# Power-of-two scales from square sums and ones-matmuls, two weights read once, and a stored rank for every operation

## Chip, cores and metric

One core of one Trainium2 chip. The metric is the device time of one launch in microseconds. The engines are TensorE (PE, its weight loads are listed as PEld), VectorE (DVE), ScalarE (ACT), GpSimd (POOL) and the queue of SyncE (SP), which issues most DMAs.

## What is computed

Three stages follow each other on 8 sequences of 576 tokens, 512 wide.

```python
scores = q @ k.T / sqrt(64)             # 8 batches, 8 heads, 576 x 64
scores = where(block_i >= block_j, scores, -1e9)   # blocks of 64 tokens
x = softmax(scores) @ v                 # heads side by side: 576 x 512
gate = sigmoid(sum_k conv_w[k] * shift(x, 4 - k))  # 5 taps along the tokens
y = (gate * (x @ w_val)) @ w_out
xk = mu_k * y + (1 - mu_k) * prev(y)    # prev: one token earlier
xr = mu_r * y + (1 - mu_r) * prev(y)
out = sigmoid(xr @ w_r) * (square(relu(xk @ w_k)) @ w_v)
```

q, k, v and the two mu are float32, the five weights float64. w_val, w_out and w_r are 512x512, w_k is 512x1024, w_v is 1024x512.

## The kernel before

**Numbers.** Every product is taken three times in float16: each operand is scaled by a power of two, split into a high and a low half (h, l), and h·l, l·h and h·h are added in PSUM. So each operand needs a bound from which its power of two is taken. `layer` (line 1086) issues such a product, in weight pieces of 64 columns (line 1095).

**Pairs.** Attention works on 32 pairs of heads, four to a batch (p = 0 to 31). `attention_in` (line 947) loads q and k of a pair, `scales` (line 833) finds the bounds, `split` (line 865) makes the halves, a DMA transpose and two DMA copies put them in place. `attention_s` (line 991) does nine score tiles: matmuls (897), row maximum on DVE (903), exponential on ACT (906), then the probabilities in halves (584, 582, 594), and a DMA transpose. `attention_out` (line 1033) multiplies by v (942), then the five taps on DVE (1049), and splits x.

**Bounds before.** For q and k of a pair the sum of absolute values of each partition is taken, on ACT or DVE (826, 828), for v a sum of squares on ACT (847). `spread` (line 614) takes the maximum over the partitions to all of them: a matmul against the float32 identity (622), a maximum on DVE (624), a small diagonal (597), a matmul with ones (628). Bit operations (600, 605), a limit, a reciprocal and a last scaling give the scale. Each chunk's xk goes the same way with one column (from line 1205).

**Weights.** A block is 128 rows x 512 columns; there are 28: 4 of w1 (w_val), 4 of w2 (w_out), 8 of w3 (w_k), 4 of wr, 8 of wv. A block of float64 comes in as pairs of 32-bit words into one of four staging places (parts of tg and xx). It is made float32 by one scaling (`rescale`, 582 or 584) and three integer steps on DVE (650, 652, 656). For w1, w2 and w3 (`weights_by_sum`, line 731) the float32 block is stored, its absolute values (742) are summed over the rows by matmuls with ones (744), and the maximum gives the scale; then come a scaling, the high half (line 727) and the subtraction that makes the low half (591). For wr and wv, `bound_of_max` (line 756) reads each block and takes a maximum on DVE (610, into wmx); after the fourth pair `weights_by_max` (line 782) reads every block a second time and scales it within the first conversion step.

**Chunks.** After attention the tokens go in 13 chunks of 384 or 192 through `chunk` (line 1119): V (x by w1), O (by w2), Z (by wr), K (by w3) and W (by wv), all on PE, with their splits on the other engines.

**Order of the work.** Nothing is issued where it is written: `plan.add` records each operation with a label, a rank, a cost, the engines that may do it, and what it reads and writes. `Plan.order` (line 78) walks through a model of the engines: on each one that is free it starts the ready operation of the lowest rank, on an operation's preferred engine (table PREF), or on another one once it has waited for its patience (PATIENCE). `plan` (line 245) did this three times, and took the ranks of the second and third from `latest` (line 201), which walks backwards from the end, plus offsets by label and some nudges. Labels with a prime belong to the first pairs and first chunks (`plan.mark`, line 1358). Each engine's instructions, and the DMAs of each queue, stand in the order so found.

Of the kernel before, what the change touches and what calls it, by code (L numbers as in the profile page):

```python
# [7 lines left out]
F32 = mybir.dt.float32  # L8
# [24 lines left out]
class Plan:  # L33
# [5 lines left out]
    MODE = {"S": 1, "pv": 1, "xT": 2, "xB": 3}  # L39
    BANKS = {"sp": (0, 1), "xps": (2,), "xt": (2, 2), "xb": (2, 2), "fp": (3, 4, 5)}  # L40
# [37 lines left out]
    def order(self, off={}, patience={}, pref={}, base=None, stay=0.0):  # L78
# [6 lines left out]
        rank = [((base[n] if base else o[1]) + off.get(o[0], 0.0), n) for n, o in enumerate(ops)]  # L85
# [50 lines left out]
        for _ in ops:  # L136
            while True:
# [10 lines left out]
                if ops[n][6] == 2:  # L148
# [3 lines left out]
            n = min((rank[x][0] + (stay if e == PE and mode[x] != last else 0.0), x)  # L152
                    for x, r in waiting[e].items() if r <= t and when(x, r, e) <= t)[1]
# [44 lines left out]
        self.span = [o[2][0][1] if o[6] else finish[n] - start[n] for n, o in enumerate(ops)]  # L198
        return sorted(range(len(ops)), key=lambda n: (start[n], n))

    def latest(self):
        ops, finish, TO = self.ops, self.finish, self.TO
        where = [SP if o[6] else e for o, e in zip(ops, self.taken)]
        users = [[] for _ in ops]
        for n, o in enumerate(ops):
            for d in o[3]:
                users[d].append(n)
        left = [len(u) for u in users]
        free = {e: 0.0 for e in (PE, DVE, ACT, POOL, SP, None)}
        waiting = {e: {} for e in free}  # L210
        back = [0.0] * len(ops)

        def ready(n):
            t = float(self.DMA_OUT) if ops[n][6] else 0.0
            for u in users[n]:
                if where[n] == where[u] == PE:
                    x = back[u] - self.DRAIN
                else:
                    x = back[u] + (0 if ops[n][6] or where[n] is None else TO[where[u]]) + (self.DMA_SET if ops[u][6] else 0)
                t = max(t, x + (self.DMA_OUT if ops[n][6] else 0))  # L220
            waiting[where[n]][n] = t

        for n in range(len(ops)):
            if not left[n]:
                ready(n)
        for _ in ops:
            best = None
            for e, w in waiting.items():
                if w:
                    t = max(free[e], min(w.values()))  # L230
                    if best is None or t < best[0]:
                        best = (t, e)
            t, e = best
            n = -min((self.end - finish[x], -x) for x, r in waiting[e].items() if r <= t)[1]
            del waiting[e][n]
            back[n] = t + self.span[n]
            free[e] = t + (self.span[n] - self.DRAIN if e == PE else max(60.0, self.span[n] - self.OVER.get(e, 0.0)))
            for d in ops[n][3]:
                left[d] -= 1
                if not left[d]:  # L240
                    ready(d)
        end = max(back)
        return [end - x for x in back]

    def plan(self):
# [1183 lines left out]
```

## Time and profile before

| | us |
|---|---|
| median of 3 runs (1041.07 to 1041.95) | 1041.94 |
| the profiled execution | 1043.63 |
| its span, first to last instruction | 1041.8 |
| PE busy | 887.8 (85%) |
| DVE busy | 860.8 (83%) |
| ACT busy | 696.8 (67%) |
| POOL busy | 556.1 (53%) |
| mean granted clock of PE | 0.966 |

Read it by stages: busy shares over the whole span hide that the engines take turns in being full. 1.00 of the granted clock is 2.4 GHz, 0.5 is 1.2 GHz.

### The profile page before, as it was taken

How to read it: one execution, taken by the hardware profiler on the slowest of the kernel's cores; microseconds unless marked ns; L12 is line 12 of the kernel's file. 1: busy time of each engine (PE TensorE's matmuls, PEld its weight loads, DVE VectorE, ACT ScalarE, POOL GpSimd, SP SyncE). 2: the span in 40 equal slices, each digit the busy share in tenths (PEclk: the TensorE clock that was granted, in tenths of full speed). 3: DMA queues.
4: the chain of work that ended last, by engine and by line, in shares of the span. 5: the costliest groups of instructions: out<-in, count | busy, mean ns of one | idle time of the engine just before them, and what ended most of it. 6: DMA issues, size and time to landing. Idle time of an engine off the chain costs nothing.

```text
span 1041.8 us, 31117 instructions
## 1 busy us (share of the span) xinstructions
PE 887.8 (85%) x12195; PEld 628.3 (60%) x12195; DVE 860.8 (83%) x2095; ACT 696.8 (67%) x1607; POOL 556.1 (53%) x1097
## 2 busy tenths in 40 slices
PE   1335337999988999999998999999999989999998
PEld 0122226667666776756665767676666867675774
DVE  5899899999999998688898996878999986866341
ACT  3758577767878777567686876577787764652431
POOL 3655655645566746366466464355667462652321
PEclk9996568999999999999999999999999999999999
DMA  7988996267987985277976946349789860440000
GB/s 238 221 248 210 218 229 166 57 128 169 178 171 149 181 147 103 58 131 152 167 136 147 185 93 118 84 111 199 146 152 166 164 130 11 113 85 12 12 22 26
DMA packets 417203, 141.51 MB, mean 136 GB/s; under 512 B 403488, under 2 KB 403488, under 8 KB 417056
## 3 DMA queue, kind: packets, MB, share of 16 engines
q1 hardware_dynamic: 414368, 130.08, 61.2%
q0 software_dynamic: 2688, 9.45, 2.7%
q8 instruction: 95, 1.56, 0.7%
q14 instruction: 52, 0.43, 0.1%
HBM read 49.31 MB, written 9.44 MB: 56 GB/s over the span
## 4 chain that ended last, share of the span: by engine, by line
PE 42%; DVE 17%; DMA 5%; ACT 4%; issue 3%; POOL 2%; SPq 1%; ACTq 0%; DVEq 0%; POOLq 0%
PE fp L1095 35%; DVE P L594 3%; PE xps L942 3%; DVE tg L1049 3%; DVE smalls L903 2%; DMA rawq<-in_q_dram 2%; PE spa L897 2%; PE spb L897 1%; DMA q2T<-qkT 1%; POOL smalls L597 1%; ACT P L906 1%; DVE kx L594 1%; DMA PT<-P 1%; DVE natqk L594 1%; DVE tmp L1280 1%
## 5 line engine op out<-in xcount | busy, mean ns | idle before, releaser
L1095 PEld LDWEIGHTS <-w 128*64 128x64 f16 x5280 | 311.3, 110 | 94.5 <-issue 16.5
L597 POOL TENSOR_SCALAR smalls<-smalls 128x1 f32<-128x1 f32 (+2 forms) x535 | 190.1, 360 | 227.2 <-DVE smalls L903 98.4
L1095 PEld LDWEIGHTS <-kx 128*64 128x64 f16 x2592 | 164.6, 110 | 107.0 <-issue 11.0
L1095 PE MATMUL fp<-wv,kx 128*64 128x512 f16 x1728 | 211.3, 379 | 2.9 <-DVE th L1300 1.9
L1095 PE MATMUL fp<-kx,w 128*64 128x384 f16 (+1 forms) x2496 | 201.0, 314 | 6.4 <-DVE tmp L1280 5.3
L591 POOL TENSOR_TENSOR kx<-tmp,kx 128x384 f16<-128x384 f32 (+1 forms) x149 | 136.9, 923 | 79.5 <-ACT kx L582 70.2
L594 DVE SCALAR_TENSOR_TENSOR P<-P,smalls,P 128x384 f16<-128x384 f32 (+8 forms) x288 | 168.8, 600 | 7.9 <-ACT P L582 4.3
L906 ACT ACTIVATE P<-spb,smalls 128x64 f32<-128x64 f32 (+4 forms) x160 | 91.0, 570 | 52.3 <-POOL smalls L597 34.0
L1095 PE MATMUL fp<-gg,w 128*64 128x385 f16 (+1 forms) x1248 | 104.7, 319 | 6.2 <-DVE tmp L1197 4.5
L1095 PE MATMUL fp<-wr,kx 128*64 128x512 f16 x864 | 106.2, 380 | 3.9 <-DVE th L1300 3.2
L1049 DVE SCALAR_TENSOR_TENSOR tg<-xps,smalls,tg 128x575 f32<-128x575 f32 (+3 forms) x128 | 102.9, 804 | 6.5 <-ACT xx L582 4.4
L1095 PE MATMUL fp<-xx,w 128*64 128x384 f16 (+1 forms) x1536 | 103.7, 287 | 3.3 <-DVE tmp L1157 2.0
L906 ACT ACTIVATE P<-spa,smalls 128x192 f32<-128x192 f32 (+3 forms) x128 | 85.3, 666 | 26.4 <-POOL smalls L597 18.9
L897 PEld LDWEIGHTS <-qkT 128*64 128x64 f16 x640 | 47.4, 114 | 84.3 <-issue 63.1
L584 POOL TENSOR_SCALAR P<-P,smalls 128x256 f16<-128x256 f32 (+4 forms) x162 | 87.0, 546 | 18.2 <-DVE smalls L264 15.7
L942 PEld LDWEIGHTS <-natv 128*64 128x64 f16 x2880 | 80.7, 116 | 15.9 <-issue 12.0
L1280 DVE SCALAR_TENSOR_TENSOR tmp<-fp,tmp 128x384 f32<-128x384 f32 (+1 forms) x104 | 53.9, 521 | 38.6 <-ACT tmp L1274 38.1
L942 PE MATMUL xps<-PT,natv 128*64 128x128 f16 (+1 forms) x2700 | 74.3, 215 | 10.6 <-DMA PT<-P 10.5
L582 ACT ACTIVATE P<-P,smalls 128x320 f16<-128x320 f32 (+8 forms) x125 | 72.4, 612 | 11.3 <-DVE smalls L264 7.3
L897 PE MATMUL spb<-qkT 128*64 128x64 f16 (+4 forms) x320 | 47.0, 297 | 34.4 <-ACT P L906 25.7
L903 DVE TENSOR_REDUCE smalls<-spb 128x1 f32<-128x64 f32 (+4 forms) x160 | 66.5, 427 | 9.3 <-PE spb L897 8.7
L903 DVE TENSOR_REDUCE smalls<-spa 128x1 f32<-128x192 f32 (+3 forms) x128 | 69.9, 546 | 4.0 <-PE spa L897 2.4
(179 smaller groups left out, 1478.2 us busy)
## 6 DMA issues: line engine op xcount, KB each, us to landing
out_dram<-th SPq DMA_DIRECT2D x35, 256.0 KB, 2.5
rawq<-in_q_dram SPq DMA_DIRECT2D x31, 288.0 KB, 3.6
rawk<-in_k_dram SPq DMA_DIRECT2D x31, 288.0 KB, 3.7
q2T<-qkT SPq DMA_DIRECT2D x60, 144.0 KB, 2.9
rawv<-in_v_dram SPq DMA_DIRECT2D x64, 128.0 KB, 2.9
xx<-in_moe_w_v_dram POOLq DMA_DIRECT2D x6, 512.0 KB, 3.8
tg<-in_moe_w_k_dram SPq DMA_DIRECT2D x4, 512.0 KB, 4.5
xx<-in_moe_w_k_dram SPq DMA_DIRECT2D x4, 512.0 KB, 7.0
```

Of the source, the lines that this page charges most:

```text
L582: nc.scalar.activation(out=o, in_=i, func=AF.Copy, scale=scale)
L584: nc.gpsimd.tensor_scalar(out=o, in0=i, scalar1=scale, scalar2=1.0, op0=ALU.mult, op1=ALU.mult)
L591: eng[e].tensor_tensor(out=o, in0=a, in1=b, op=ALU.subtract)
L594: nc.vector.scalar_tensor_tensor(out=o, in0=a, scalar=scale, in1=b, op0=ALU.mult, op1=ALU.subtract)
L597: eng[e].tensor_scalar(out=o, in0=i, scalar1=a, scalar2=b, op0=op0, op1=op1)
L897: nc.tensor.matmul(sp[64 * h:64 * h + 64, c0:c1], qts[e][:, S * h + 64 * u:S * h + n], kt[:, S * h + c0:S * h + c1], start=(e == 0), stop= ...
L903: nc.vector.tensor_reduce(out=mx, in_=sp, op=ALU.max, axis=AX.X)
L906: nc.scalar.activation(out=P[:, 0:n], in_=sp, func=AF.Exp, scale=small["posc"][p % 3], bias=nb, accum_out=sm)
L942: nc.tensor.matmul(xps[r:r + 64, 128 * i:128 * i + 64 * m].rearrange("p (a c) -> p a c", c=64), w, PT[:, a:a + 2 * (m - 1) * (i + 1) + 1:2 ...
L1049: lambda t=t: nc.vector.scalar_tensor_tensor(out=acc[:, t:S], in0=ps[:, 0:S - t], scalar=cx[:, 4 - t:5 - t], in1=acc[:, t:S], op0=ALU.mult ...
L1095: nc.tensor.matmul(o[a:a + 64], w[:, a:a + 64], y, start=(k == i == j == 0), stop=(k == nk - 1 and i == len(ps) - 1), skip_group_check=True)
L1280: nc.vector.scalar_tensor_tensor(out=t, in0=fp, scalar=2.0 ** -21, in1=t, op0=ALU.mult, op1=ALU.mult)
```

## The change

- **q, k, v.** All three bounds are sums of squares on ACT, written as bfloat16 (`squares`). A matmul per bound takes the 128 partition sums, spread over 128 columns, against a 0/1 matrix `fours` that adds four partitions each; the result stands on all partitions, DVE takes the maximum of the 32 groups. One bit operation (`root`), one limit, one reciprocal: two of the steps before are gone.
- **xk of a chunk.** The partition maxima are squared and summed by a matmul with ones.
- **Weights.** One function, `weights`, for all five. w_r and w_v are read once, stored as float32 in the place of their own halves, bounded by a sum of squares on ACT, and scaled through two spare buffers before the halves are written over them. Their layout changes to high and low side by side for each block. The scaling of these 12 blocks is now an operation of its own.
- **First integer step.** `top_bits` can run on ACT or DVE; on ACT it is an activation on the upper 16 bits with a pointer operand as bias.
- **Order.** `latest`, the offsets and the nudges are gone. A table RANKS holds one rank for every single operation, and `order` runs once. The tables of preferences and patience are new: in the first part of the kernel the subtractions of w1, w2, wr and wv (labels w1o, w2o, wro, wvo) prefer DVE (before: DVE, DVE, POOL, POOL), the scaling of w1 and w2 (w1p, w2p) DVE (before POOL and ACT), the conversion of wv POOL (before ACT), the high half of k (hik) ACT (before DVE), the copies swap0 POOL (before DVE), the step w1x and wrx ACT, wvx DVE; w2x, w3x and wvp have no entry and take the first engine of their list, ACT.
- Powers of two in later scales are adapted. Some code for cutting the first batch in two is there, with one cut only (`CUTS = [0, S]`), so that pairs and chunks are the same as before.

The core of the diff:

```diff
-        rank = [((base[n] if base else o[1]) + off.get(o[0], 0.0), n) for n, o in enumerate(ops)]
+        rank = [(base[n], n) for n in range(len(ops))]
...
     def plan(self):
-        self.order(OFF, PATIENCE, PREF)
-        for _ in range(ITER):
-            self.order(OFF2, PATIENCE, PREF, self.latest(), STAY)
-        base = self.latest()
-        seen = {}
-        for n, o in enumerate(self.ops):
-            seen.setdefault(o[0], []).append(n)
-        for lab, a, b, ns in NUDGE:
-            for n in seen.get(lab, ())[a:b]:
-                base[n] += ns
-        return self.order(OFF3, PATIENCE3, PREF3, base, STAY3)
+        count, base = {}, []
+        for o in self.ops:
+            i = count.get(o[0], 0)
+            count[o[0]] = i + 1
+            base.append(10.0 * RANKS[o[0]][i])
+        return self.order(PATIENCE, PREF, base)
...
+RANKS = {
+    'K': [25939, 23255, 23589, 29719, 31190, 30355, 29139, 30364, 30768, 30882, 31013, 31071, 31842, 32349,
...
+    def mm(o, w, y, start=True, stop=True):
+
+        for a in range(0, w.shape[-1], 64):
+            nc.tensor.matmul(o[a:a + 64], w[:, a:a + 64], y, start=start, stop=stop, skip_group_check=True)
...
+    def top_bits(e, raw):
+
+        if e == DVE:
+            narrow(raw, 0)
+        else:
+            up = raw.bitcast(mybir.dt.uint16)[..., 1:2].rearrange("p n w -> p (n w)")
+            nc.scalar.activation(out=raw[..., 0], in_=up, func=AF.Identity, scale=2.0 ** -13, bias=half)
...
-            for j in range(3):
+            add(lab + "x", rank + 0.6, {DVE: c_ts(n, 0)[DVE], ACT: c_ts(n, 0)[ACT] + 96}, [ACT, DVE], key + ["ones"], key,
+                lambda e: top_bits(e, raw), share=True)
+            for j in range(1, 3):
                 last = j == 2 and o is not None
-                add(lab, rank + 0.6, c_tt(n) if j else c_ts(n, 0), [DVE], key, list(okey) if last else key,
+                add(lab, rank + 0.6, c_tt(n), [DVE], key, list(okey) if last else key,
                     lambda j=j, last=last: narrow(raw, j, o.bitcast(I32) if last else None), share=True)
...
+        bp = xps[:, 968 + 8 * (a - 4):968 + 8 * (a - 4) + nb]
+        add(nm + "l", rank, 60, [PE], [("l2w", nm, i) for i in range(nb)] + ["ones"], [("xb", 2 + a)],
+            lambda: mm(bp, ones, l2w[:, a, 0:nb]))
+        add(nm + "s", rank, 160, [DVE], [("xb", 2 + a)], [("wl", nm)],
+            lambda: nc.vector.tensor_reduce(out=wl, in_=bp, op=ALU.add, axis=AX.X))
+        add(nm + "s", rank, 170, [DVE], [("wl", nm)], [("wg", nm)], root, wg, wl)
+        add(nm + "s", rank, SM, PD, [("wg", nm)], [("wa", nm)], lambda e: ts2(e, wa, wg, 2.0 ** 88, TINY, ALU.mult, ALU.max))
+        add(nm + "s", rank, 160, [DVE], [("wa", nm)], [("wr1", nm)], nc.vector.reciprocal, ws, wa)
+        add(nm + "s", rank, SM, PD, [("wr1", nm)], [("ws", nm)],
+            lambda e: ts2(e, ws, ws, scaled, 1.0, ALU.mult))
+        return ws
...
+            def norm(t=t, i=i):
+                with nc.allow_low_precision(reason="a sum of squares that a power of two is taken of"):
+                    nc.scalar.activation(out=aw, in_=t, func=AF.Square, scale=2.0 ** -24, accum_out=l2w[:, a, i:i + 1])
+
+            add(nm + "a", rk + 1, 285 + 0.84 * WCH, [ACT], tkey, ["aw", ("l2w", nm, i)], norm)
         rk = rank + len(blocks) * step + 1
-        s = scale_of(nm, rk)
...
+            o, okey = temps[i % len(temps)] if temps else (t, tkey)
+            add(nm + "p", rk + 0.4 * i, c_ts(WCH), ANY, list(tkey) + [("ws", nm)], list(okey), lambda e, t=t, o=o: ts(e, o, t, s), share=True)
+            h, l = (x[..., c0:c0 + WCH] for x in halves(r))
+            split_weight(nm, rk + 0.4 * i + 0.2, o, okey, h, l, [(nm, r, c0 // 512)], list(extra), tkey if temps else ())
...
+    def squares(p, c, src):
+        with nc.allow_low_precision(reason="a sum of squares that a power of two is taken of"):
+            nc.scalar.activation(
+                out=junk[:, 0:src.shape[1]], in_=src, func=AF.Square, scale=2.0 ** -24, accum_out=l2[:, p % 2, c:c + 1])
...
+        def gather():
+            for c in range(c0, c1):
+                mm(bp[:, c], l2[:, i2, c:c + 1].broadcast_to([128, 128]), fours)
+
+        add("xS", r, 150, [PE], lk + ["ones"], [("xb", i2)], gather)
+        add("par", r, 150 + 33 * (c1 - c0), [DVE], [("xb", i2)], [("pb", i2)],
+            lambda: nc.vector.tensor_reduce(out=pb[:, c0:c1], in_=bp[:, c0:c1], op=ALU.max, axis=AX.X))
+        add("par", r, 165, [DVE], [("pb", i2)], [("pb", i2)], root, pb[:, c0:c1], pb[:, c0:c1])
+        add("pc", r, SM, PD, [("pb", i2)], [("pc", i2)],
+            lambda e: ts2(e, pc[:, c0:c1], pb[:, c0:c1], 2.0 ** 74, QMIN * 2.0 ** -14, ALU.mult, ALU.max))
...
-        yk, yg = spread(r, 1, [("yx", iy)], yx)
-        add("ysc", r, 170, [DVE], [yk], [("py", iy)], bits, py, yg)
+        y2, yg = l2[:, iy, 3:4], xps[:, 964 + iy:965 + iy]
+
+        def squared(e):
+            with nc.allow_low_precision(reason="a sum of squares that a power of two is taken of"):
+                ts2(e, y2, yx, 2.0 ** -24, yx, ALU.mult)
+
+        add("ysc", r, SMA, PD, [("yx", iy)], [("y2", iy)], squared)
+        add("xS", r, 60, [PE], [("y2", iy), "ones"], [("xb", 2 + iy)], lambda: mm(yg, ones, y2))
+        add("ysc", r, 170, [DVE], [("xb", 2 + iy)], [("py", iy)], root, py, yg)
         add("ysc", r, 160, [DVE], [("py", iy)], [("sk", iy)], nc.vector.reciprocal, sk, py)
-        add("ysc", r, SM, PD, [("sk", iy)], [("sk", iy)], lambda e: ts2(e, sk, sk, 2.0 ** 13, 1.0, ALU.mult))
+        add("ysc", r, SM, PD, [("sk", iy)], [("sk", iy)], lambda e: ts2(e, sk, sk, 2.0 ** -61, 1.0, ALU.mult))
...
-            weights_by_sum("w3", w_k, w3, DFF, u_wv, 28, 2.5, ["free3"])
-            bound_of_max("wr", w_r, KD, DM, 50, 1.5)
-            bound_of_max("wv", w_v, KF, DM, 56, 1.5)
+            add("free3", 0, 0, [None], [], [("raw1", x, y) for x in range(2) for y in range(4)] + [("nat1", x, y) for x in range(3) for y in range(2)] + ["free3"], lambda: None)
+            weights("w3", w_k, planes(w3), KD, DFF, u_wv, 28, 2.5, extra=["free3"])
+            weights("wr", w_r, rows(wr), KD, DM, u_wr, 50, 2.5, spare)
...
-        if p == HP:
-            add("freev", 0, 0, [None], [], [("u_wv", i) for i in range(8)] + ["freev"], lambda: None)
-            weights_by_max("wr", w_r, wr, KD, DM, zp(HP) + 8, 2)
-            weights_by_max("wv", w_v, wv, KF, DM, zp(HP) + 24, 1.5, ["freev"])
```

## Rows read from the trace of the kernel before

**Rows 1.** Windows by stage: stretch, its length, busy us (count) by engine, clock, DMA share, GB/s.

```profile
0.00:26.00 26.00, 3.61 (x8) 0.80 (x9) 14.94 (x37) 9.80 (x17) 10.02 (x28) 1.00 0.74 238
26.00:208.00 182.00, 95.02 (x1143) 63.56 (x1144) 172.29 (x416) 128.45 (x291) 110.22 (x168) 0.81 0.81 193
208.00:300.00 92.00, 83.75 (x1261) 60.94 (x1258) 85.84 (x232) 67.33 (x166) 45.40 (x106) 1.00 0.77 156
300.00:900.00 600.00, 570.05 (x8061) 408.09 (x8059) 521.81 (x1265) 437.24 (x1016) 343.79 (x718) 1.00 0.68 133
900.00:1042.00 142.00, 135.38 (x1734) 94.94 (x1728) 65.96 (x150) 53.98 (x120) 46.68 (x78) 0.99 0.18 44
```

**Rows 2.** Page, strips of 40 slices: granted clock of PE, busy share of the DMA engines.

```profile
PEclk9996568999999999999999999999999999999999
DMA  7988996267987985277976946349789860440000
```

**Rows 3.** Groups by line and shape, DVE, 0 to 182 us: xcount | busy us, mean ns | idle before.

```profile
L650 DVE TENSOR_SCALAR xx<-xx 128x512 int32<-128x512 int32 x12 | 6.2, 513 | 1.1 <-DMA xx<-in_moe_w_val_dram 1.1
...
L650 DVE TENSOR_SCALAR tg<-tg 128x512 int32<-128x512 int32 x12 | 4.9, 417 | 6.1 <-DMA tg<-in_moe_w_val_dram 6.1
...
L828 DVE TENSOR_REDUCE smalls<-rawk 128x1 f32<-128x576 f32 x4 | 2.9, 736 | 0.0
...
L610 DVE TENSOR_REDUCE wmx_wv<-xx 128x1 f32<-128x512 f32 x4 | 2.7, 671 | 0.0
...
L828 DVE TENSOR_REDUCE smalls<-rawq 128x1 f32<-128x576 f32 x3 | 2.2, 745 | 0.5 <-DMA rawq<-in_q_dram 0.5
...
L610 DVE TENSOR_REDUCE wmx_wr<-tg 128x1 f32<-128x512 f32 x2 | 1.4, 706 | 0.5 <-DMA tg<-in_moe_w_r_dram 0.5
```

**Rows 4.** DMA issues by line: KB of each, us from issue to landing.

```profile
xx<-in_moe_w_v_dram POOLq DMA_DIRECT2D x6, 512.0 KB, 3.8
```

**Rows 5.** Groups by line and shape, DVE, 0 to 182 us.

```profile
L588 DVE TENSOR_SCALAR natqk<-rawk,smalls 128x576 f16<-128x576 f32 x5 | 4.0, 805 | 0.0
...
L591 DVE TENSOR_TENSOR w<-xkf,w 128x512 f16<-128x512 f32 x2 | 1.4, 686 | 0.7 <-ACT w L582 0.7
...
L588 DVE TENSOR_SCALAR xkf<-xkf,smalls 128x512 f32<-128x512 f32 x2 | 0.9, 475 | 0.0
...
L586 DVE COPY natv<-natqk 128x576 f16<-128x576 f16 x2 | 0.6, 322 | 0.2 <-ACT natqk L582 0.2
```

**Rows 6.** Groups by line and shape, ACT, 0 to 182 us.

```profile
L742 ACT ACTIVATE junk<-wv 128x512 bf16<-128x512 f32 x8 | 5.0, 623 | 1.5 <-DVE smalls L597 0.7 <-PE fp L744 0.7
...
L582 ACT ACTIVATE xx<-xx 128x512 f32<-128x512 f32 x6 | 4.0, 669 | 1.3 <-DMA xx<-in_moe_w_k_dram 1.0 <-DMA xx<-in_moe_w_out_dram 0.3
...
L582 ACT ACTIVATE natqk<-rawq,smalls 128x576 f16<-128x576 f32 x5 | 3.8, 766 | 4.2 <-POOL smalls L597 4.2
...
L582 ACT ACTIVATE wv<-wv,smalls 128x512 f32<-128x512 f32 x5 | 3.4, 708 | 0.0
...
L847 ACT ACTIVATION_READ_ACCUMULATOR junk<-rawv 128x1 f32 x6 | 1.1, 192 | 0.0
```

**Rows 7.** Windows of line 622 alone: length, PE busy us (matmuls), PEld, clock, DMA.

```profile
208.00:1042.00 834.00, 14.46 (x76) 3.37 (x76) 1.00 0.61 120
```

**Rows 8.** Timeline of PE, 224 to 236 us: start, us, engine line, tiles, count.

```profile
224.80 0.20 PE L897 MATMUL spb<-qkT 128*64 128x64 f16 x2
...
224.86 0.23 PE L897 MATMUL spb<-qkT 128*64 128x128 f16 x2
...
228.47 0.38 PE L622 MATMUL xps<-ident,smalls 128*1 128x128 f32 x2
228.78 0.30 PE L897 MATMUL spb<-qkT 128*64 128x256 f16 x2
...
235.92 0.17 PE L628 MATMUL xps<-diag,ones 3*128 3x3 bf16 x1
```

**Rows 9.** Page, costliest groups: xcount | busy us, mean ns | idle before.

```profile
L1095 PEld LDWEIGHTS <-w 128*64 128x64 f16 x5280 | 311.3, 110 | 94.5 <-issue 16.5
```

More of the change, by code (lines that the diff above doesn't have):

```diff
@@ L76, in transpose, with order @@
         self.add(lab, rank, self.BLOCK * blocks, [SP], reads, writes, fn, *args, dma=2)
[L78 removed]
+    def order(self, patience, pref, base):
         ops, TO, OVER = self.ops, self.TO, self.OVER
@@ L151, in order @@
             t, e = best
-            n = min((rank[x][0] + (stay if e == PE and mode[x] != last else 0.0), x)
-                    for x, r in waiting[e].items() if r <= t and when(x, r, e) <= t)[1]
+            n = min(rank[x] for x, r in waiting[e].items() if r <= t and when(x, r, e) <= t)[1]
             for f, _ in ops[n][2]:
@@ L729, in split_weight @@
-        add(lab + "o", rank + 0.3, c_tt(n), [POOL, DVE], list(key) + extra + kh, kl, lambda e: sub(e, l, val, h), share=True)
-    def weights_by_sum(nm, src, dst, width, store, rank, step, extra=(), queues=QS):
-        blocks = [(c0, r) for c0 in range(0, width, WCH) for r in range(KD)]
+        add(lab + "h", rank, c_ts(n, 0), ANY, list(key) + extra, kh + list(over), lambda e: ts(e, h, val), share=True)
+        add(lab + "o", rank + 0.3, c_tt(n), [POOL, DVE], list(key) + extra + kh, kl + list(over), lambda e: sub(e, l, val, h), share=True)
@@ L734, in weights_by_sum, with weights @@
+    def weights(nm, src, halves, nk, width, store, rank, step, temps=(), extra=(), queues=QS):
+        blocks = [(c0, r) for c0 in range(0, width, WCH) for r in range(nk)]
         a, _ = wcol[nm]
@@ L844, in scales @@
         if p:
             vi = (p - 1) % RING["rawv"]
-            add("l1v", r, 285 + 0.84 * NV * D, [ACT], [("rawv", vi, x) for x in range(3)], [("l1", i2, 2)] + (["aw"] if p < 7 else []),
-                lambda: nc.scalar.activation(out=junk, in_=rawv[vi], func=AF.Square, scale=2.0 ** -24, accum_out=l1[:, 2:3]))
-        xk_, bp = spread(r, 3, [("l1", i2, c) for c in range(3)], l1)
-        add("par", r, 170, [DVE], [xk_], [("pb", i2, 0)], bits, pb[:, 0:2], bp[:, 0:2])
-        add("par", r, 170, [DVE], [xk_], [("pb", i2, 1)], root, pb[:, 2:3], bp[:, 2:3])
@@ L1059, in batch_scale @@
+        add("gate", r + 3.5, c_act(n), [ACT], ak, ak,
+            lambda: nc.scalar.activation(out=acc[:, q0:q1], in_=acc[:, q0:q1], func=AF.Tanh, scale=0.5))
+    def batch_scale(b, t0, t1):
+        z = zp(LAST[b + NS - 1 if b else CUTS.index(t0)] + 1) + 4
         i2, i4, sl = b % 2, b % 4, b % 2
```

778 lines of the change are left out of this document (409 added, 369 removed), and 384 rows, old and new, of tables (NUDGE, OFF, OFF2, OFF3).

## Prediction

> **What bounds the kernel now.** I read the windows by stage first, then the strips of the page, then the groups by line inside the first stage. All durations are from the profiled execution: span 1041.8 us, its own time 1043.63 us, against a median of 1041.94 us of the three timed runs; I make the sum against 1043.63 and take off 1.7 at the end.
>
> The windows [rows 1] show two kernels in one. From 208 us on TensorE (PE) is busy 83.75 + 570.05 + 135.38 = 789.2 of 834 us, 94.6%, at a granted clock of 1.00, with VectorE (DVE) at 81% (85.84 + 521.81 + 65.96 = 673.6). That part is bound by PE. Before it PE is busy 98.6 of 208 us, and DVE 14.94 + 172.29 = 187.2: in 26 to 208 us DVE is busy 95% of the time, ScalarE (ACT) 71%, POOL 61%. The start is bound by DVE, which narrows the float64 weights while it serves the first pairs and the first chunk. The strips [rows 2] add two things: the 16 DMA engines are nearly as full there (tenths 9, 8, 8, 9, 9, 6 in slices 2 to 7), and the clock falls to tenths 5 to 6 in slices 4 to 6, where PE has gaps; PE is not the limit there, so that costs little.
>
> So a microsecond of DVE work taken out of the start is worth about a microsecond, and a microsecond of PE work taken out later nearly as much. Work on ACT, POOL or the DMA engines alone is hidden, up to the point where one of them becomes the limit.
>
> **Removed from DVE in the start** [rows 3]. (a) The first reading of w_r and w_v: 12 maxima of 128x512; of the four groups the first and last have 671 and 706 ns: 12 x 0.68 = 8.2 us. (b) The sums of q and k that DVE took, 4 of 736 and 3 of 745 ns: 5.2 us; all go to ACT. (c) The first integer step. It has a choice now, and its preference is ACT for w1, w2, w3 and w_r, 20 of the 28 blocks, and DVE for w_v. The rows give 417 ns undisturbed and 513 with one stretched instruction among them: 20 x 0.417 = 8.3 us. Together 21.7 us.
>
> **Removed from the DMA engines** [rows 4]. 12 of the 24 transfers of 512 KB for w_r and w_v (seven rows such as the one shown, 24 issues): 6.3 MB, at the 193 GB/s of 26 to 208 us 33 us of transfer. In the start DVE hardly waits for DMA, so I count 0; it only makes sure that the DMA engines are not next in line. Taken away from their queues are also 12 issues, on SP and POOL.
>
> **Put onto DVE or taken off it by the new preferences** [rows 5]. The subtraction that makes a weight's low half now prefers DVE for w1, w2, w_r and w_v, 20 blocks; in the trace DVE did 4 (two rows of 2, at 686 ns) and 2 of w_v around 200 us: 14 x 0.686 = +9.6. The scaling of w1 and w2 prefers DVE, 8 against 3: 5 x 0.475 = +2.4. The high half of k in the first pairs goes from DVE to ACT, 5 x 0.805 = -4.0; the swapped copies to POOL, four (two rows of 2) at 0.32 = -1.3. Net +6.7. A preference only binds as long as its patience lasts, so this is the softest term: its bounds are 0 (the subtractions stay on POOL and only the two removals count, then -5) and +12.
>
> The scale chain of a pair keeps its DVE share: one reduction, two bit steps and a reciprocal before, one reduction, one bit step, one limit and a reciprocal after. It loses three POOL steps; no price.
>
> DVE in the start: -21.7 + 6.7 = **-15 us**, between -27 and -10 by DVE alone.
>
> **Put onto ACT** [rows 6]. 20 first steps at 0.71 (nearest row: 128x512 with a pointer operand, 708 ns) = 14.2; 12 squares of w_r and w_v at 0.623 + 0.192 for the accumulator = 9.8; 7 squares of q and k by the same rows (576 columns, a little more) = 5.7; 5 high halves at 0.766 = 3.8; the separate scaling of w_v, 8 x 0.708 = 5.7; the rescaling of w_v prefers POOL, 8 x 0.669 = -5.4. Net +34 us: 9.80 + 128.45 = 138.3 [rows 1] becomes 172. In a start of 208 - 15 = 193 us that is 89%, where DVE is at 172.2, also 89%. The cover holds, but barely: ACT's idle time in the start falls from 70 to 21 us. I take 0.
>
> **PE.** A maximum across partitions cost two fp32 matmuls and one small matmul. After 208 us there are 76 / 2 = 38 of them [rows 7], 12 for chunks (13 less the first), 26 for pairs. On PE's timeline [rows 8] the pair holds the array for 228.78 - 228.47 = 0.31 us and the small one for at most 0.17: about 0.42 together. In their place stand six matmuls of 32 columns for a pair and two of one column for a chunk. Bounds: six at the pace of the four 64-column ones at 224.80 (0.06 us for four) are 0.09 us; six that each wait for a weight load of 110 ns [rows 9] are 0.66, longer than what they replace. I take 0.2 for a pair and 0.1 for a chunk, nearer to the 64-column row because they are the same kind: 26 x 0.22 + 12 x 0.32 = 9.6 us. As PE is busy 94.6% and other engines hold the rest, I count two thirds: **-6 us**, between -14 (0.09 and 0) and +4 (0.66 and 0.22).
>
> **Order.** All positions are new: one stored rank per operation in place of a computed one. From 208 us on PE idles 44.8 us; one point of idle share is 8.3 us, either way. I count 0 and let the range carry it.
>
> Sum: 1043.6 - 15 - 6 = 1022.6 for a profiled execution, **1021 us** for the median.
>
> **Rivals.**
> 1. The start shrinks further: the subtractions stay on POOL as their patience ends, and DVE loses 27 us, or PE fills better: 1042 - 27 - 6 = 1009, with a point less idle 1001. For: POOL is idle 39% of 26 to 208 us. Against: the lists ask for DVE. Chance 0.17.
> 2. The DVE time is hidden after all: the start's length is set by the chain of loads, scales and transposes of the first five pairs, not by DVE's sum, and only PE's part counts: 1036. For: PE waits there for ACT and for transposes in turn. Against: DVE is busy 95% without a break over 182 us. Chance 0.12.
> 3. Slower: ACT becomes the limit of the start. Its 34 us are added to an engine that the first pairs' exponentials also need in order; if half of it falls outside ACT's 70 us of idle time, the start grows by 17 instead of shrinking by 15: 1042 + 17 - 6 = 1053. It decides from the point where more than 6 of the 34 us fall outside the idle time: then PE's part is used up. For: ACT's gaps are short and tied to arrivals. Against: the sums above leave DVE and ACT equal at 89%. Chance 0.11. The Trainium skill, page "ScalarE: Activation LUTs", section "Rules for kernel authors", speaks for this rival: additions and multiplications belong on VectorE, not ScalarE. By it the moved step alone would go from 8.3 to 14.2 us; the rows agree with its direction (417 against 708 ns), but it weighs one instruction, not which engine is the limit.
> 4. The change does not do what it says, because the order of before had already hidden all of it, or the new order gives the gain back later: 1042, half a point of idle share around it. Chance 0.10.
>
> **How the numbers follow.** The forecast has 0.50, its own range 1009 to 1031. About 0.2% (2 us) is what a measurement of this kernel can tell from no change. Faster by more: forecast 0.50, rival 1 0.17, rival 2 0.12 and half of rival 4's spread, about 0.05: 0.84. Slower: rival 3 with the rest of the order's risk, 0.11. Same: 0.05. The range from 1000 to 1037 holds the forecast, most of rival 1 and rival 2, and leaves out rivals 3 and 4.
>
> **What would show it.** In the profile after: PE's lasting 9s in the strip begin about half a slice earlier (near 193 instead of 208 us); 12 maxima, 7 reductions and some 20 first steps are gone from DVE's groups; DVE at about 172 and ACT at about 173 us by then; the DMA strip under 8 in slices 2 to 6; 128x3 transposes gone from PE. I am wrong if the start is as long as before with ACT at 95% or more, if PE's idle share after the start moves by more than a point, or if the small matmuls take more than 0.4 us a pair.

## The result and the profile after

The changed kernel takes **1029.74 us** (median of 4 runs, 1027.66 to 1032.14) where the kernel before, run beside it, takes 1041.51 us: a ratio of 0.988 [0.9857, 0.9902], 12 us faster. The forecast was 1021 in a range of 1000 to 1037. The direction came out, the size is little more than half, and the reason given for most of it does not hold. The profile below is of the slowest of the four runs, 1032.14 us.

The page of the changed kernel, busy time by engine and two of its strips, stands against [rows 2]:

```profile
span 1030.4 us, 31105 instructions
...
PE 876.7 (85%) x12289; PEld 666.5 (65%) x12289; DVE 839.1 (81%) x2027; ACT 731.3 (71%) x1693; POOL 478.8 (46%) x946
...
PEclk9995569999999999999999989999999999999999
DMA  9999957576959874365778886659658963230000
GB/s 245 208 213 236 205 103 126 121 156 132 170 114 178 181 167 103 91 129 129 138 150 156 166 123 137 133 109 170 111 106 173 166 128 71 55 76 12 11 22 27
DMA packets 417090, 135.22 MB, mean 131 GB/s; under 512 B 404912, under 2 KB 404912, under 8 KB 416944
```

DVE gave up 21.7 us over the span, ACT took on 34.5 (696.8 before, 731.3 now), which is the forecast's +34. The transfers fell from 141.51 to 135.22 MB, the 6.3 MB of the first reading. But the DMA strip stays at 9 in slices 1 to 5 (counted from 1, as in the prediction): the weights are now fetched earlier, the last transfer of w_v is issued at 117.98 us instead of 190.65.

Windows of the kernel before and then of the changed one, in stretches of 26 us (stretch, its length, busy us and count of PE, PEld, DVE, ACT and POOL, granted clock, DMA share, GB/s):

```profile
78.00:104.00 26.00, 13.42 (x148) 7.25 (x147) 25.94 (x70) 22.91 (x52) 13.96 (x28) 0.63 0.87 209
104.00:130.00 26.00, 9.35 (x148) 6.47 (x149) 22.19 (x56) 13.48 (x30) 18.11 (x31) 0.59 1.06 217
130.00:156.00 26.00, 8.62 (x133) 6.42 (x133) 24.93 (x63) 19.88 (x47) 14.98 (x27) 0.67 1.03 231
182.00:208.00 26.00, 23.40 (x321) 17.65 (x316) 25.37 (x57) 19.08 (x39) 16.48 (x20) 1.00 0.20 57
```

```profile
78.00:104.00 26.00, 10.77 (x134) 6.93 (x134) 24.23 (x53) 23.09 (x52) 18.21 (x28) 0.57 1.16 242
104.00:130.00 26.00, 9.38 (x120) 6.53 (x120) 24.88 (x54) 25.40 (x62) 15.79 (x23) 0.57 0.91 194
130.00:156.00 26.00, 12.55 (x179) 9.74 (x180) 21.68 (x50) 20.10 (x43) 13.75 (x15) 0.65 0.55 102
182.00:208.00 26.00, 25.15 (x384) 20.91 (x382) 22.89 (x55) 18.77 (x43) 15.01 (x25) 0.99 0.57 120
```

The first fence says what the one window of 26 to 208 us in [rows 1] hid, because its last 26 us have a DMA share of only 0.20: from 104 to 156 us the 16 DMA engines are full (1.06 and 1.03), while in 104 to 130 us DVE has 3.8 us to spare. In the second, the DMA engines are full earlier (1.16 in 78 to 104 us) and 130 to 156 us stands at 0.55; in between, DVE and ACT are the fullest: 24.88 and 25.40 of 26 us.

Windows of the kernel before and of the changed kernel, before and after 208 us:

```profile
0.00:208.00 208.00, 98.63 (x1151) 64.35 (x1153) 187.23 (x452) 138.25 (x307) 120.24 (x195) 0.84 0.80 199
```

```profile
0.00:208.00 208.00, 104.09 (x1277) 70.94 (x1279) 181.66 (x441) 172.96 (x389) 106.64 (x182) 0.84 0.88 181
208.00:1028.00 820.00, 772.57 (x11016) 595.53 (x11012) 657.39 (x1587) 558.33 (x1304) 372.13 (x765) 0.99 0.60 119
```

From these the change of the span can be added up on PE. By 208 us it has done 104.09 - 98.63 = 5.5 us more; its work over the span is 887.8 - 876.7 = 11.1 us less; after 208 us it idles 1030.4 - 208 - 772.6 = 49.8 us against 44.6, 5.2 more (6.1% against 5.4%; the prediction's 44.8 rounds the span of 1041.8 us up to 1042). 5.5 + 11.1 - 5.2 = 11.4 us, which is 1041.8 - 1030.4. So the start gave a third of what was forecast for it, and nearly half of PE's saving went into idle time.

### The profile page after: what moved, and what is told of

Its sections match the earlier page's. It is cut to its first block, busy times and chain, and to the rows that moved or that the text cites. A ratio compares the mean times of both kernels' runs of the same rounds, so it can differ in the third digit from the quotient of the medians.

```text
span 1030.4 us, 31105 instructions
## 1 busy us (share of the span) xinstructions
PE 876.7 (85%) x12289; PEld 666.5 (65%) x12289; DVE 839.1 (81%) x2027; ACT 731.3 (71%) x1693; POOL 478.8 (46%) x946
## 2 busy tenths in 40 slices
DMA packets 417090, 135.22 MB, mean 131 GB/s; under 512 B 404912, under 2 KB 404912, under 8 KB 416944
## 5 line engine op out<-in xcount | busy, mean ns | idle before, releaser
L869 PEld LDWEIGHTS <-w 128*64 128x64 f16 x5280 | 328.5, 111 | 80.2 <-issue 18.1
L891 POOL TENSOR_SCALAR smalls<-smalls 128x1 f32<-128x1 f32 (+1 forms) x467 | 161.1, 348 | 280.5 <-DVE smalls L1223 146.8
L869 PEld LDWEIGHTS <-kx 128*64 128x64 f16 x2592 | 180.5, 111 | 103.4 <-issue 14.6
L888 DVE SCALAR_TENSOR_TENSOR P<-P,smalls,P 128x512 f16<-128x512 f32 (+8 forms) x288 | 162.2, 573 | 11.5 <-ACT P L876 5.9
L885 POOL TENSOR_TENSOR kx<-tmp,kx 128x384 f16<-128x384 f32 (+1 forms) x140 | 126.0, 902 | 81.9 <-ACT kx L876 67.6
L1226 ACT ACTIVATE P<-spb,smalls 128x128 f32<-128x128 f32 (+4 forms) x160 | 91.1, 570 | 45.1 <-POOL smalls L891 35.6
L878 POOL TENSOR_SCALAR P<-P,smalls 128x192 f16<-128x192 f32 (+5 forms) x146 | 80.4, 559 | 22.3 <-DVE smalls L213 21.2
L876 ACT ACTIVATE P<-P,smalls 128x320 f16<-128x320 f32 (+7 forms) x138 | 79.5, 600 | 12.8 <-DVE smalls L213 6.6
L1217 PE MATMUL spa<-qkT 128*64 128x192 f16 (+4 forms) x320 | 55.8, 316 | 34.2 <-ACT P L1226 33.7
L1223 DVE TENSOR_REDUCE smalls<-spa 128x1 f32<-128x192 f32 (+3 forms) x128 | 70.4, 550 | 13.6 <-PE spa L1217 10.6
L1223 DVE TENSOR_REDUCE smalls<-spb 128x1 f32<-128x128 f32 (+4 forms) x160 | 67.3, 429 | 14.2 <-PE spb L1217 13.3
```

What stands on the lines that cost most here:

```text
L869: nc.tensor.matmul(o[a:a + 64], w[:, a:a + 64], y, start=start, stop=stop, skip_group_check=True)
L876: nc.scalar.activation(out=o, in_=i, func=AF.Copy, scale=scale)
L878: nc.gpsimd.tensor_scalar(out=o, in0=i, scalar1=scale, scalar2=1.0, op0=ALU.mult, op1=ALU.mult)
L885: eng[e].tensor_tensor(out=o, in0=a, in1=b, op=ALU.subtract)
L888: nc.vector.scalar_tensor_tensor(out=o, in0=a, scalar=scale, in1=b, op0=ALU.mult, op1=ALU.subtract)
L891: eng[e].tensor_scalar(out=o, in0=i, scalar1=a, scalar2=b, op0=op0, op1=op1)
```

## The experiments

Twelve kernels ran, each 6 to 12 times. Times differ more between runs of one kernel here than the forecast assumed: the changed kernel run again had 1029.72 to 1036.82 us. Beside each ratio to the kernel before stands a second measure, taken ahead of places that add to this spread (last section): when, in the one profiled execution, PE starts the first product with w_v, the last layer of chunk 0. The two profiles of the changed kernel, 198.98 and 200.45 us, show how far it varies by itself. The measure compares kernels of one order only: in the changed kernel the product comes 14.2 us earlier than before, but by then PE has done 95.1 us of work and not 103.8, so the new order has put other work behind it.

| kernel | median us | ratio to before | first product with w_v, us |
|---|---|---|---|
| before | 1040.9 to 1041.5 | 1 | 213.16 |
| b_once | 1037.13 | 0.9953 [0.9932, 0.9974] | 206.31 |
| b_nomax | 1041.87 | 1.0007 [0.9992, 1.0021] | 211.83 |
| b_step_act | 1043.99 | 1.0016 [0.9994, 1.0038] | 214.24 |
| b_l1_act | 1043.65 | 1.002 [1.0007, 1.0033] | 212.05 |
| b_gather | 1040.18 | 0.9974 [0.9954, 0.9995] | 212.66 |
| changed | 1029.74 | 0.988 [0.9857, 0.9902] | 198.98 |
| a_again | 1031.5 | 0.9913 [0.9889, 0.9937] | 200.45 |
| a_gather2 | 1032.79 | 0.9905 [0.9878, 0.9932] | 199.63 |
| a_nosq | 1029.18 | 0.9883 [0.9859, 0.9906] | 197.00 |
| a_sub_pool | 1033.88 | 0.9932 [0.9911, 0.9953] | 201.29 |
| a_step_dve | 1035.52 | 0.9941 [0.9921, 0.996] | 202.81 |
| a_max12 | 1035.48 | 0.994 [0.9916, 0.9963] | 204.01 |
| a_order_old | 1052.47 | 1.011 [1.009, 1.013] | 227.06 |

Names with b are edits of the kernel before, names with a edits of the changed one. Except for a_order_old, all operations keep the positions that they had in the kernel that was edited.

### a_again: the changed kernel once more

No edit.

> The changed kernel once more, as the base of the other three. All theories: ratio to before 0.988, within 0.986 to 0.990, some 1029.5 us.

Measured 0.9913 [0.9889, 0.9937], which lies outside the 0.986 to 0.990 expected and overlaps the first measurement's interval only at its edge. I take the two together as 0.988 to 0.991, 9 to 12 us.

### b_once and b_nomax: the first reading, with and without its transfers

The first leaves out 12 transfers and 12 maxima, the second the maxima alone.

```diff
-            raw, key = load_weight(nm + "m", rank + r * step, src, r, 0, width, early, 0, [], queues, sn)
-            add(nm + "m", rank + r * step + 1, 150 + 1.04 * width, [DVE], key, [("wm", nm, r)], amax, wmx[nm][:, r:r + 1],
-                raw[..., 1].bitcast(F32) if wide else raw)
+            raw, key = load_weight(nm + "m", rank + r * step, src, r, 0, width, early, 0, [], queues, sn, False)
+            add(nm + "m", rank + r * step + 1, 150 + 1.04 * width, [DVE], key, [("wm", nm, r)], lambda: None)
...
-            lambda: nc.vector.tensor_reduce(out=wl, in_=wmx[nm][:, 0:nk], op=ALU.max, axis=AX.X))
+            lambda: nc.vector.memset(wl, 1.95 if nm == "wr" else 1.5))
```

(`False` leaves the transfer out; b_nomax has the two other edits only.)

> The kernel before, order held, without its first reading of w_r and w_v: 12 transfers of 512 KB and 12 maxima of 128x512 on DVE (8.2 us) are left out, the maximum is set as a constant. Theory 1, DVE's sum sets the start: 8 us faster, about 1033.5. Theory of a chain of loads, scales and transposes that DVE's work fills: 0 to 3 us faster. If the DMA engines limit as well: more than 10 us faster.

> The kernel before with its order held, all 12 first transfers of w_r and w_v kept, only the 12 maxima (8.2 us of DVE) left out; the two bounds are constants, so the output can differ from the reference by the scales of w_r and w_v. It splits the 4.9 us that the kernel without the whole first reading gained. Theory 1 (DVE's time in the start): the same gain with the transfers in place, -4 to -6 us, about 1036.5. Theory 2 (the transfers were what counted, as they stand ahead of the weights in the queues): at most -2 us, 1039.5 or more. Between the two: both.

b_once gains 4.9 us (0.47% of 1041), b_nomax nothing. That is less than the 8 us of theory 1 and more than the 0 to 3 of the chain's theory. Between the two kernels lie only the transfers: 1.0007 - 0.9953 = 0.54%, 5.6 us. **As long as the transfers were there, the 8.2 us of maxima on DVE were free; it was the 33 us of transfers, which the forecast counted as 0, that had to go.** The other half, the transfers gone and the maxima kept, was not run on the kernel before. In the changed kernel, where the transfers are gone, the same maxima cost something (a_max12 below), so the 4.9 us may need both, and the split by 0 and 5.6 holds for this order of taking away. What became of DVE's freed time stands in the waits of DVE of b_nomax, 95 to 150 us (engine, line, what it waited for: us in total, times, longest):

```profile
DVE smalls L827 <- DMA rawq<-in_q_dram: 6.1, 1, 6.1
```

DVE had finished and stood 6.1 us for the q of the next pair; the kernel before has its maxima to do meanwhile, waits 2.5 us for a transfer of w_v among them, and comes to that q without a wait. Where that transfer stands, on SP's timeline of the kernel before, then of b_nomax, then of b_once (start, us, line, tiles; q is line 578):

```profile
98.48 0.74 SPq L694 DMA_DIRECT2D tg<-in_moe_w_v_dram  x1
99.31 7.65 SPq L878 DMA_TRANSPOSE qkT<-natqk  x1
107.02 0.57 SPq L578 DMA_DIRECT2D rawq<-in_q_dram  x1
```

```profile
96.12 0.64 SPq L694 DMA_DIRECT2D tg<-in_moe_w_v_dram  x1
96.86 7.00 SPq L877 DMA_TRANSPOSE qkT<-natqk  x1
103.91 0.57 SPq L578 DMA_DIRECT2D rawq<-in_q_dram  x1
```

```profile
95.96 3.09 SPq L877 DMA_TRANSPOSE qkT<-natqk  x1
99.10 0.58 SPq L578 DMA_DIRECT2D rawq<-in_q_dram  x1
```

In b_nomax q is issued 3.1 us earlier than before, and its sum on DVE starts at 112.19 us instead of 113.09: the transfer takes 8.3 us from issue to landing instead of 4.2, with the DMA engines at 1.08, and 0.9 us is left of the gain. In b_once it is issued at 99.10, with no first reading ahead of it, and its sum starts at 106.52. The issue of w_v itself takes SP less than a microsecond; what holds q back is the transpose between them, which keeps SP's queue for 7.65 and 7.00 us with the first reading in the queues and for 3.09 without. Whether the transfers cost by filling the DMA engines or by their place in the queues was not run apart. Windows of b_nomax and of b_once:

```profile
104.00:130.00 26.00, 9.81 (x152) 6.60 (x153) 17.79 (x52) 12.34 (x30) 16.71 (x30) 0.60 1.08 226
130.00:156.00 26.00, 8.79 (x133) 6.76 (x133) 24.87 (x59) 19.88 (x46) 14.61 (x26) 0.66 1.01 214
```

```profile
104.00:130.00 26.00, 10.90 (x162) 7.62 (x163) 23.27 (x59) 16.82 (x39) 22.04 (x40) 0.63 0.93 219
130.00:156.00 26.00, 12.51 (x155) 8.96 (x156) 25.96 (x60) 19.40 (x46) 13.24 (x21) 0.64 0.96 201
```

Without its maxima DVE is busy 17.79 of 26 us and the DMA engines are as full as ever; without the transfers DVE works on, and in 130 to 156 us it is busy 25.96 of 26.

The Trainium skill, page "Perfetto Trace Analysis", section "Identifying the Most-Contended Engine", says to judge VectorE by its occupancy and DMA by the use of the HBM, not by occupancy; the same sentence then has the reader find which DMA resource binds. By its ranking DVE, at 95%, is the engine to relieve first, and DMA, with 56 GB/s of HBM traffic over the span of the kernel before, comes far behind. The runs speak against that order for this kernel: the relieved DVE gave nothing, and time was won by taking transfers out of a stretch in which the busy share of the DMA engines, 1.06 in 104 to 130 us, was what stood out.

### b_step_act and b_l1_act: the two other terms on DVE

The first integer step of w1, w2, w3 and w_r on ACT (20 blocks); and the sums of q and k that DVE took on ACT (7).

```diff
...
-  lambda j=j, last=last: narrow(raw, j, o.bitcast(I32) if last else None), share=True)
+  lambda j=j, last=last: narrow(raw, j, o.bitcast(I32) if last else None) if j else top_bits(raw), share=True)
...
```

```diff
-                fn(self.taken[n], *args)
+                e = self.taken[n]
+                if self.ops[n][0].rstrip("'") in ("l1q", "l1k"):
+                    e = ACT
+                fn(e, *args)
```

> The kernel before, order held, with the first integer step of 20 blocks (w1, w2, w3, w_r) on ACT: 8.3 us less on DVE, 14 us more on ACT, which is busy 71% of 26 to 208 us there. Theory 1: 6 to 8 us faster, about 1034.5. Theory 2, that ACT's waits and not its sum matter: no faster, or up to 5 us slower.

> The kernel before with its order held, the sums of q and k that DVE took (7 in the start, 5.2 us) forced onto ACT. Theory 1 (DVE's time in the start counts one to one): -4 to -5 us, 1036 to 1037.5. Theory 2 (half price, as the maxima added to the changed kernel showed): -2 to -3 us, 1038.5 to 1039.5. Theory 3 (the sum then comes later on ACT and the scale chain of the pair waits for it): 0 to +2, 1041 to 1043.

Both moves together take 13.5 us off DVE in the forecast's count; neither gains: 1.0016 [0.9994, 1.0038] and 1.002 [1.0007, 1.0033], the second 2 us slower. In b_l1_act the start is 1.1 us shorter by the first product with w_v, and that is gone by the end. In b_step_act, line 664 is the step on ACT, and DVE's next step on the block (line 652) waits for it:

```profile
L664 ACT ACTIVATE tg<-tg,half x10: 740/747/771, 6.4 to 145.9; 128x512 int32<-128x512 uint16 x10
L664 ACT ACTIVATE xx<-xx,half x10: 727/748/771, 12.3 to 153.3; 128x512 int32<-128x512 uint16 x10
...
  DVE tg L652: 7.2, 2
  DVE xx L652: 3.5, 3
```

(The first two lines: ns min/median/max, first and last start in us; the last two: who waited for it, us and times.) 10.7 us of such waits are more than the 8.3 us that left DVE. In an unchanged order the moved step became a wait for ACT's place in line, so these two runs show what the moves are worth in the old order, and not what DVE's time alone is worth.

### a_step_dve, a_max12, a_sub_pool, a_nosq: what DVE and ACT are worth after the change

All first integer steps back on DVE; the 12 maxima added; the 16 subtractions of weights that DVE does in the start forced onto POOL; the 12 squares of w_r and w_v left out, with constants in place of the sums.

```diff
...
+                e = self.taken[n]
+                lab = self.ops[n][0].rstrip("'")
+                if lab in ("w1x", "w2x", "w3x", "wrx", "wvx"):
+                    e = DVE
...
```

```diff
+    def also(lab, raw, j):
+        if j == 1 and lab in ("wr", "wv"):
+            amax(wmx[:, extra[0]:extra[0] + 1], raw[..., 1].bitcast(F32))
+            extra[0] += 1
...
```

```diff
...
+                if lab in ("w1o'", "w2o'", "w3o'", "wro'", "wvo'"):
+                    e = POOL
...
```

```diff
+        nc.vector.memset(l2w[:, a, 0:nb], 2.0 ** -48 if nm == "wr" else 2.0 ** -49)
...
-                    nc.scalar.activation(out=aw, in_=t, func=AF.Square, scale=2.0 ** -24, accum_out=l2w[:, a, i:i + 1])
+                    pass
```

> The changed kernel with its planned order held, the first integer step of all 28 blocks on DVE: 25 activations of 0.75 us leave ACT, 25 steps of 0.42 us (10.5 us) come to DVE. Theory 1, DVE's sum sets the length of the start: 8 to 10 us slower than the changed kernel, about 1039. Theory 2, ACT has become the limit of the start (98 of 104 us busy between 26 and 130 us): faster by 3 to 10 us, about 1023. If both engines limit in turn: within 3 us.

> The changed kernel, order held, with the 12 maxima of 128x512 put back on DVE ahead of the second integer step of w_r and w_v (8.2 us of DVE work in the start, nothing else). Theory 1, DVE's sum sets the start: 7 to 8 us slower, about 1037. Theory 2, ACT sets it: 0 to 3 us slower.

> The changed kernel with its order held, the 16 subtractions of weights that its preferences put on DVE in the start (11.5 us of DVE at 0.68 to 0.80 us) forced onto POOL (1.15 to 1.3 us each, about +19 us on an engine that is busy 53% there). My forecast took these as +9.6 us of DVE and of time. Theory 1 (DVE is the one limit of the start, near one to one): -8 to -11 us against the changed kernel, 1020 to 1023. Theory 2 (DVE and ACT share the limit, 0.4 to 0.5 us per us of DVE): -4 to -6, 1025 to 1027. Theory 3 (the new preferences are right, POOL's longer subtraction comes late to the transposes and products that need it): 0 to +5, 1030 to 1036.

> The changed kernel with its order held, the 12 sums of squares of w_r and w_v on ACT left out (12 x about 0.8 = 9.8 us of ACT); the sums are constants, so the output can differ by a power of two in the scales. Theory 1 (only DVE counts in the start, ACT's added time is covered, as my forecast had it): within 1.5 us of the changed kernel, 1029 to 1032. Theory 2 (ACT has become a limit beside DVE): -3 to -6 us, 1024 to 1028, and the wait of 12 us of PE at 121 to 133 us for the bound of w_v gone or far shorter.

More work on DVE now costs something. The 12 maxima (8.2 us) move the first product with w_v to 204.01 us, 3.6 later than in a_again and 5.0 later than in the first profile; in the time it is 0.994 against 0.988 to 0.9913, 3 to 6 us. The steps back on DVE (10.5 us) move it 2.4 to 3.8 us later and give the same ratio within the interval. That is about half a microsecond for one of DVE, not one. The intervals of either and of a_again overlap, so the time alone would not settle it; the start moves the same way in both, by more than the 1.5 us between the two profiles of the changed kernel.

The subtractions taken off DVE (11.5 us) do not shorten the start; it is 0.8 to 2.3 us longer, and the time is 1033.88, 2 to 5 us above the changed kernel by the ratios, with intervals that overlap a_again's. So the preference that my forecast entered as +9.6 us costs nothing that can be seen: on POOL the same subtraction takes 1.2 to 1.4 us in the mean, against 0.68 to 0.80, and comes later to what needs it.

Leaving out 9.8 us of squares on ACT changes the time (1029.18) by 0 to 3 us, which its spread covers, and brings the first product with w_v to 197.00 us, 2.0 to 3.5 earlier. That shift is nearly as large as the one that the steps on DVE made, so by the start ACT is worth something too, a fifth to a third of a microsecond for one; it is not shown that ACT's time is free. PE's longest wait of this part, which the profile puts down to ACT, is there in both. PE's timeline of the changed kernel (start, us, line, tiles, idle time before and its releaser), and of a_nosq:

```profile
133.28 0.22 PE L869 MATMUL xps<-l2w,ones 128*64 128x8 bf16 x2 [12.01 <-ACT junk L1075]
...
140.13 4.21 PE L1267 MATMUL xps<-kx,natv 128*64 128x128 f16 x90 [4.13 <-DVE natv L888]
```

```profile
127.25 0.22 PE L869 MATMUL xps<-l2w,ones 128*64 128x8 bf16 x2 [9.45 <-DVE tg L1396]
132.62 0.35 PE L869 MATMUL xps<-fours,l 128*64 128x32 bf16 x6 [5.15 <-DVE smalls L1038]
138.74 4.10 PE L1268 MATMUL xps<-kx,natv 128*64 128x128 f16 x90 [5.78 <-DVE natv L888]
```

With the squares PE waits 12.01 us for the bound of w_v; without them it waits 9.45 + 5.15 us for DVE, and the product after it starts 1.4 us earlier.

### b_gather and a_gather2: the bound across partitions on PE

The new way across the partitions, for the bounds of the pairs alone, in the kernel before; and the six small matmuls of each pair issued twice in the changed one.

```diff
...
+            def gather():
+                for k in range(3):
+                    for a in (0, 64):
+                        nc.tensor.matmul(gp[a:a + 64, k], src[:, k:k + 1].broadcast_to([128, 128])[:, a:a + 64], fours,
+                                         start=True, stop=True, skip_group_check=True)
...
```

```diff
-            for c in range(c0, c1):
+            for c in list(range(c0, c1)) * 2:
```

> The kernel before, order held, with the new way across the partitions for the 33 bounds of the pairs only: six small matmuls and one reduction in place of two fp32 matmuls, a reduction, a diagonal and a matmul with ones; sums as before. As forecast: 26 x 0.22 us less on PE after the start, two thirds of it 4 us faster, about 1037.5. If other engines set the pace between the matmuls: within 1 us of before. If each small matmul waits for its weight load: 4 us slower.

> The changed kernel, order held, with every group of six small matmuls issued twice: prices one group. As forecast (0.2 us a pair, two thirds of it on PE's path): 26 x 0.2 x 2/3 = 3.5 us slower than the changed kernel. If they are hidden in PE's gaps: 0 to 1. If each weight load of 110 ns shows: 26 x 0.66 = 17 us, two thirds of it 11.

b_gather: PE's busy time falls from 887.8 to 875.6 us, 12.2 less, and the time by 2.7 us (0.9974 [0.9954, 0.9995]). It also takes the small diagonal and the matmul with ones out of each pair's chain. Groups of PE, of the changed kernel and of a_gather2:

```profile
L869 PE MATMUL xps<-fours,l 128*64 128x32 bf16 x192 | 10.5, 191 | 21.6 <-ACT junk L1143 19.9 <-DVE tg L1395 1.2 <-DVE smalls L894 0.5
```

```profile
L869 PE MATMUL xps<-fours,l 128*64 128x32 bf16 x384 | 13.8, 189 | 18.6 <-ACT junk L1143 16.6 <-DVE tg L1395 1.4 <-DVE smalls L894 0.5
```

Six matmuls keep PE busy for 10.5 / 32 = 0.33 us a pair, and 192 more of them add 3.3 us in all; the time does not move. In front of them PE has stood idle 21.6 us, nearly all of it for ACT's sums, so their length is hidden behind that wait. The 2.7 us of b_gather may then come from the shorter chain as much as from PE's time; that was not run apart.

### a_order_old: the changed operations in the order of before's planner

The stored ranks replaced by the earlier method, with its offsets, preferences and patience (labels that are new keep their entries).

```diff
...
-        return self.order(PATIENCE, PREF, base)
+        return self.order(OFF3, PATIENCE3, PREF3, base, STAY3)
```

> The operations of the changed kernel, ordered by the method, offsets and preferences of before (new labels keep the new preferences). Theory that the stored ranks carry the gain: 1040 or more. Theory that the removed work carries it: within 5 us of 1029.5. If the stored ranks cost something after the start, below 1027.

1052.47 us, 11 slower than before, 21 slower than a_again. PE's longest wait in 60 to 230 us is the same bound of a weight as above, at twice the length:

```profile
PE xps L625 <- ACT junk L831: 22.8, 1, 22.8
PE xps L1023 <- DVE natv L644: 14.8, 2, 10.4
```

With the old tables the new operations lose. The old offsets, preferences and nudges were fitted to the old operations, and the new labels have no offset at all, so this prices those tables for the new operations and not stored ranks as such. It doesn't say what new ranks for the old operations would be worth either; that was not tried.

## Why the prediction was right in direction and wrong in size

- **"So a microsecond of DVE work taken out of the start is worth about a microsecond."** This is the step that failed. In the kernel before, with its transfers in place, 8.2 us of maxima were worth 0 us. The 5.2 us of sums and 8.3 us of first steps gave no gain either, but there DVE's work became ACT's in an unchanged order. In the changed kernel a microsecond more on DVE costs about half of one. Its "busy 95% without a break over 182 us" was an average: 104 to 130 us has 22.19 of 26. A DVE so busy was taken for the limit; in the stretch that the traces show it was filling time in which the next pair's q had not come. The whole -15 us rested on it.
- **"In the start DVE hardly waits for DMA, so I count 0".** Failed the other way: with the maxima out, the transfers gave 5.6 us, about half of the 9 to 12. DVE hardly waited because its maxima lay in the gap: without them it waits 6.1 us for q. [rows 2] showed the tenths 9 and 9 in slices 5 and 6 and I called them "nearly as full"; I priced a window that averaged them with an empty stretch.
- **New preferences, "Net +6.7".** DVE does take them, 16 subtractions in the start, but their price was wrong: forced onto POOL they do not shorten the start, and the ratios are 0.2 to 0.5% higher, not clear of the spread. The preferences for w1 and w2 stood in the last tables of before as well.
- **ACT, +34 us, "I take 0".** Right in size, 34.5 us more. Its price is near 0 in the time: 9.8 us taken off again give 0 to 3 us, though the start moves by 2.0 to 3.5. Rival 3 had ACT's filling right (97.91 of 104 us in 26 to 130, 94%) and its consequence wrong. For the moved step itself the Trainium skill, page "ScalarE: Activation LUTs", section "Rules for kernel authors", which gives additions and multiplications to VectorE, agrees with the rows: it is slower on ACT, 0.75 against 0.417 us. With the steps back on DVE the changed kernel took 1035.52 us against 1031.5, which such a rule for one instruction cannot say.
- **PE, "-6 us".** Right in kind, a little large. For the pairs alone the forecast's two thirds of 26 x 0.22 is 3.8 us; 2.7 was measured, part of it perhaps from the shorter chain. Six matmuls took 0.33 us and not 0.2. The chunks' part was not run by itself.
- **Order, "I count 0".** With the old tables the new operations take 21 us more than with the stored ranks, so the order is not free. If the two parts add, which was not run, the held-order runs explain 4.9 + 2.7 = 7.6 of 9 to 12 us; the rest, 1 to 5, belongs to order, preferences and the chunk bounds together, and was not taken apart.
- **The clock, no term at all.** After 208 us the sum takes PE at its full granted clock, as before. In the changed kernel the clock falls there again and again (last section). What that cost in time was not run.
- **The signs to look for.** DVE and ACT by 193 us were given as 172 and 173; by the windows they are 167.7 and 163.7. PE's full stretch does begin earlier (25.15 of 26 us in 182 to 208), and the 12 maxima and 7 sums are gone; ACT does 25 of the 28 first steps, not 20. The idle share moved by 0.7 points, within the bound given. The DMA strip stayed at 9 in slices 2 to 5 and fell to 5 only in slice 6, against the sign; it was the sign that pointed at the wrong step.

Rival 2 came nearest: DVE's time was hidden by the chain of loads. It gave 1036, because it too counted the transfers as nothing. That the time fell inside the range is in good part luck: two errors of opposite sign, DVE's price and DMA's.

## What to carry to other kernels

Cut the windows where a resource's own strip changes, before naming the limit of a stage: an average of 0.81 held two stretches above 1.0 and one at 0.20. Call a busy engine the limit only if taking work from it starts the next thing earlier; ask what the freed engine would wait for, and look for that transfer's place in the queue. Of a change that leaves out reading, computing and storing together, price the reading first where the DMA engines are full.

## What the runs showed that I had not expected

**One place where runs of one kernel part.** Around 580 to 600 us PE has a gap, and after it the granted clock may fall or not. Windows of the changed kernel, then of a_again:

```profile
580.00:590.00 10.00, 4.83 (x126) 3.95 (x120) 8.01 (x17) 8.03 (x18) 2.91 (x8) 1.00 0.87 174
590.00:600.00 10.00, 9.52 (x178) 8.44 (x179) 9.97 (x30) 6.75 (x18) 4.34 (x10) 1.00 0.99 157
```

```profile
580.00:590.00 10.00, 6.13 (x154) 4.95 (x152) 7.91 (x19) 7.63 (x19) 3.90 (x12) 1.00 1.12 210
590.00:600.00 10.00, 8.35 (x141) 7.98 (x137) 8.74 (x23) 4.64 (x13) 1.36 (x4) 0.66 0.53 111
```

The same 48 matmuls of a chunk's first layer after the gap took 2.17 us in the one (from 590.24) and 4.05 us in the other (from 592.42), the difference between the levels of 2.4 and 1.2 GHz. From there to the end a_again stays 4 to 5 us behind, of which 1.5 to 2.2 were there before the gap. A comparison of a few microseconds at this kernel's end can so be decided by one gap of PE, far from the edit. It is not the whole spread: the runs of the kernel before lie as far apart (1037.91 to 1047.70 us), and its profile has no such fall.

**The changed kernel loses clock after the start.** In stretches of 10 us from 210 to 1020 us, the clock of the kernel before is 1.00 in every one. That of the changed kernel is 0.83 in those from 270, 300, 360 and 830 us and 0.66 in the second of these two, after gaps of PE of 0.82 and 1.18 us:

```profile
600.00:610.00 10.00, 8.72 (x160) 6.24 (x158) 9.70 (x19) 9.78 (x29) 6.92 (x14) 1.00 0.85 136
610.00:620.00 10.00, 7.28 (x52) 3.69 (x53) 9.84 (x30) 7.33 (x16) 6.23 (x11) 0.66 0.70 94
```

Summed as (1 - clock) times the length, that is 10.2 us, in a_again 13.6, in the other held-order edits of the changed kernel 6.8 to 13.6, in a_order_old 6.7, in the edits of the kernel before 0 to 3.4. The mean clock of the four runs of the changed kernel is 0.956 to 0.959, that of the runs of the kernel before 0.959 to 0.969. This may be a part of why 1021 us was not reached; no run shows how much.

**A small matmul's listed duration is here not what one more of them costs:** 191 ns each in the group, but 192 more added 13.8 - 10.5 = 3.3 us of PE's busy time, 17 ns each.
